# Token shares by expert, a later conversion of weights and an earlier scaling in an attention, MoE and gated-MoE kernel

## The chip, the cores and the metric

The kernel runs on one core of a Trainium2 chip. Its engines are TensorE (PE in the rows, with PEld for its weight loads), VectorE (DVE), ScalarE (ACT), GpSimd (POOL) and SyncE (SP, which only issues transfers). The metric is the device time of one execution in microseconds (us), lower is better.

## The reference

```python
attn = softmax(q @ k.T / 8 + bias) @ v          # 2 batches, 8 heads, 576 positions, 64 wide
x = attn as (1152 tokens, 512)
x = softplus(x @ w_in) @ w_out                  # 512 -> 2048 -> 512
P = exp(logits - max); 8 times: rows, then columns of P scaled to sums 1 and N / E
for e in range(8):                              # E = 8 experts, 512 -> 1024 -> 512
    h = np.maximum(x @ w1[e], 0.0)
    out += P[:, e:e + 1] * (h @ w2[e])
```

## The kernel before

The work after the attention is cut into 40 units of 256 hidden columns each: units 0 to 7 are the first MLP, units 8 to 11 are expert 0, and each further four units are one expert more. The tokens are kept as two blocks of 512 (c = 0, 1) and a rest of 128. Tokens lie along the free dimension, so that the hidden values are [128 hidden, 512 tokens]. float32 accuracy comes from splitting every operand in a high half (rounded to fp32r, a ScalarE copy, `first`) and a low half (the rest, `second`, a subtraction on VectorE or GpSimd). Each product is three matmuls: high with high, low weight with high, high weight with low.

Units 12 to 38 (`fast(u)`) do both the up and the down projection as seven products of 2 x 2 blocks instead of eight (Strassen-Winograd). The up projection takes its products in the order `UP_FAST = (1, 2, 6, 5, 7, 3, 0, 4)` (0 is the rest of 128 tokens, `up_last`). The down projection, `down_fast(u)`, takes seven steps, `at` = 0 to 6, on the blocks B11, T1, T2, B22, T3, B21, T4 of the gated hidden values; T1 to T4 are differences of the B blocks. Products 1 and 2 of unit u + 1 are done inside `down_fast(u)`, and product 6 of unit u + 1 is the first thing after it. The hidden values of a block are multiplied by the tokens' shares for the expert (`pb[c]`, the same row on all 128 partitions) by the VectorE instruction of L880.

The order on each engine is the order of the code; nothing is reordered, and each engine waits where its next instruction has to wait. Between steps 0 and 1 of `down_fast` stand: the ScalarE conversion of the second half of the next unit's up weights (`high(u + 1, 1)`); B21's gating and its high half; at every fourth unit the loads of the next expert's shares; the difference T4; the high and low halves of T3; the low half of B21. Then come T4's halves.

With `by_dma`, a weight piece's conversion is two ScalarE copies (the high half, L730, and its negative into the low half, L734) and a DMA that GpSimd issues (L735) and that adds the float32 source to the low half. In each unit GpSimd issues four such DMAs: wu (this second half), then after `mixd` (L754) wu (the first half of the unit after next) and wd (the down weights), then room (`highs`, the sums of the down weights). All go through one queue, q0. SyncE's transfers (weights, shares) go through q1.

The shares of all tokens and experts, P, are written once to DRAM as the tile `pt` of 72 rows of 128 floats, row t * E + e for token tile t and expert e (`publish`, in unit 11). `share_of` loads 4 of the 9 token tiles of one expert on all partitions: 4 rows of 512 bytes for each. Shares are loaded in `publish` (four transfers: two for expert 1, two for expert 0) and in units 15, 19, 23, 27, 31 and 35 (two each). In unit 12 the sums of expert 0, which were taken without shares, are multiplied by expert 0's shares (`weigh_columns`, L1038: one call on VectorE at n = 3, two on GpSimd at n = 5, one on VectorE in `down_fast`, step 6), where n counts the places in `UP_FAST`.

Of the kernel before, what the change touches and what calls it, by code (L numbers as in the profile page):

```python
# [25 lines left out]
E = 8  # L26
# [87 lines left out]
def attention_moe_moe_kernel(ctx: ExitStack, tc, qT, kT, vN, wpos, w_in, w_out, w_gate, e_w1, e_w2,  # L114
                             psi, logd, rpsi, place, out):
    nc = tc.nc
# [501 lines left out]
    def experts(m0, accp, xr):  # L618
# [6 lines left out]
        U1 = F1 // 256  # L625
        UE = F2 // 256
# [4 lines left out]
        pool = {}  # L631
# [16 lines left out]
        def wd(u):  # L648
            return wds[u % 2]
# [63 lines left out]
        def mix(u):  # L713

            if u >= NU or u in PLAIN:
                return
            w, t = whole2(u, 0), fs[1]

            def at(f, off, *dims):
                return win(f, off, [*dims, [256, 2], [1, 128]])  # L720

            nc.gpsimd.tensor_tensor(out=at(t, 0, [128, 2]), in0=at(w, 128, [512, 2]), in1=at(w, 0, [512, 2]), op=ALU.subtract)
            nc.gpsimd.tensor_tensor(out=at(t, 512), in0=at(w, 640), in1=at(w, 128), op=ALU.subtract)
            nc.gpsimd.tensor_tensor(out=at(t, 640), in0=at(w, 640), in1=at(t, 0), op=ALU.subtract)
            nc.gpsimd.tensor_tensor(out=at(t, 128), in0=at(t, 0), in1=at(t, 128), op=ALU.subtract)  # L725
# [36 lines left out]
        weights = dict(m=rescale, a=convert_a, b=convert_b, c=convert_c, mix=lambda u, k: mix(u), high=high, highd=highd, mixd=mixd, highs=highs)  # L762
        wss, tss, pb = [], [], {}
# [44 lines left out]
        def product(u, n):  # L808

            if n in (1, 2, 5):  # L810
                hold["XYZ"[(1, 2, 5).index(n)]] = bank({1: "t", 2: "tail", 5: "pv"}[n])
            zz = hold[CHAIN[n]]
            xn, wn = PRODUCTS[n]
            k = 0
            for j in range(2):
                for a, b in TRIPS:
                    o = WAT[wn] + 256 * j
                    nc.tensor.matmul(zz, wu(u)[:, a, o:o + 128], xs[xn][b][j], start=(n in (1, 2, 5) and k == 0), stop=(k == 5),  # L818
                                     skip_group_check=True)
                    k += 1  # L820
# [38 lines left out]
        def second(eng, name):  # L859
            t = h[name]  # L860
            eng.tensor_tensor(out=t[:, 1], in0=full[name], in1=t[:, 0].bitcast(F32), op=ALU.subtract)  # L861

        def difference(eng, out, a, b):
            eng.tensor_tensor(out=full[out], in0=full[a], in1=full[b], op=ALU.subtract)
# [111 lines left out]
        def turn_last(u):  # L976
            zt, gl = bank("tail"), hold["gl"]
            for j in range(2):
                nc.tensor.transpose(zt[:, 128 * j:128 * j + 128], gl[:, 128 * j:128 * j + 128], ident)
            t = h["last"] = pool["moe"].tile([128, 2, 256], F32R, tag="hl", bufs=1, name="hl")  # L980
            split_h(u, t, zt[:, 0:256])
            low()

        def down_fast(u):
            product(u + 1, 1)
            begun.add((u + 1, 1))
            banks = hold["sums"]
            for at, (n, x, a, b, (c, i)) in enumerate(DOWN):
                m, o = WDAT[a]
                ws = wss if m else [wd(u)[:, 0], wd(u)[:, 1]]  # L990
                order = [(k, f) for k in range(3) for f in range(2)] if at else [(k, f) for f in range(2) for k in range(3)]
                for k, f in order:
                    wo, ho = ((0, 0), (1, 0), (0, 1))[k]
                    nc.tensor.matmul(banks[x][:, f], ws[wo][:, o + 128 * f:o + 128 * f + 128], h[b][:, ho],  # L994
                                     start=(n in (1, 5, 2) and k == 0), stop=(k == 2), skip_group_check=True)
                if u == U1 + UE and at == 6:
                    weigh_columns(nc.vector, c, i)
                for fs_ in (slice(0, 2),) if at else (slice(0, 1), slice(1, 2)):
                    d = acc[c][:, 2 * i:2 * i + 2][:, fs_]
                    nc.vector.tensor_tensor(out=d, in0=banks[x][:, fs_], in1=d, op=ALU.add)  # L1000
                if at == 0:
                    turn_last(u)
                    if u > U1 + UE:
                        weights["high"](u + 1, 1)
                    later.pop()()
                    if (u + 1 - U1) % UE == 0:
                        shares_of((u + 1 - U1) // UE)
                    difference(nc.gpsimd, "T4", "B21", "T2")
                    first("T3")
                    second(nc.gpsimd, "T3")  # L1010
                    second(nc.gpsimd, "B21")
                if at == (2 if u == U1 + UE else 0):
                    if len(tss) < 3:
                        tss.append(again(2, [128, 2, 512], F32R))
                    h["T4"] = tss[2]
                    first("T4")
                    second(nc.gpsimd, "T4")
                if at == 3:
                    after(u + 1, 1)
                if at == 2:  # L1020
                    r = last_sum(u, "pv")
                if at == 4:
                    product(u + 1, 2)
                    begun.add((u + 1, 2))
                if at == 4:
                    evac(u, 2, 0, r)
                if at == 6:
                    after(u + 1, 2)
                for what, ahead, k in DOWN_JOBS.get(at, ()):
                    if u + ahead < NU:  # L1030
                        weights[what](u + ahead, k)

        def again(n, shape, dtype):
            return (m0 if n < 2 else pool["moe"]).tile(shape, dtype, tag=f"raw{n}", bufs=1, name="raw")

        def weigh_columns(eng, c, i):
            d = acc[c][:, 2 * i:2 * i + 2]
            eng.tensor_tensor(  # L1038
                out=d, in0=d, in1=pb["first", c].rearrange("p (o n) -> p o n", o=1).to_broadcast([128, 2, 512]),
                op=ALU.mult)  # L1040
# [165 lines left out]
        NT = NTOK // 128  # L1206
# [39 lines left out]
        def publish():  # L1246

            tt, sb = bank("t"), raws[2][:, 512:640]
            nc.tensor.transpose(tt[0:NT * E, 0:128], pool["prob"].rearrange("p t e -> p (t e)"), ident)
            nc.vector.tensor_copy(sb[0:NT * E], tt[0:NT * E, 0:128])  # L1250
            nc.sync.dma_start(out=pool["pt"], in_=sb[0:NT * E])
            pb["first", 0], pb["first", 1] = raws[2][:, 0:512], fs[2][:, 512:1024]
            for c in range(2):
                share_of(1, c)
                nc.sync.dma_start(out=pb["first", 1 - c].rearrange("p (t n) -> p t n", n=128), in_=shares(0, 4 * (1 - c), 4))

        def shares(e, t, n):
            src = pool["pt"][:]
            return bass.AP(tensor=src.tensor, offset=src.offset + (t * E + e) * 128, ap=[[0, 128], [128 * E, n], [1, 128]])

        def share_of(e, c):
            pb[c] = pool["moe"].tile([128, 512], F32, tag=("s3", "lgt")[c], bufs=1, name="pb")
            nc.sync.dma_start(out=pb[c].rearrange("p (t n) -> p t n", n=128), in_=shares(e, 4 * c, 4))

        def shares_of(e):
            for c in range(2):
                share_of(e, c)
# [96 lines left out]
        def unit(u):  # L1364
# [62 lines left out]
            if u == U1:  # L1427
                first_up(jobs)
            else:
                for n, p in enumerate(UP_FAST if fast(u) else UP):  # L1430
                    if u == U1 + UE and n == 5:
                        tss.extend(again(k, [128, 2, 512], F32R) for k in range(2))
                        for i in range(2):
                            weigh_columns(nc.gpsimd, 0, 1 - i)
                    if n == 3 and u == U1 + UE:
                        weigh_columns(nc.vector, 1, 0)
                    if n == 6 and u == U1 + UE:
                        weights["high"](u + 1, 1)
                    if n > 1:
                        ask(u, f"q{n - 2}" if n < 5 else f"r{n - 5}")  # L1440
                    if p:
                        do(u, p)
                    else:
                        up_last(u)
                    if u > U1 + UE and p in (6, 5):
                        weights["highs"](u, (6 - p,))
                        if p == 5:
                            weights["mix"](u + 1, 0)
                    jobs(n)
# [222 lines left out]
```

## Time and profile before

| | us |
|---|---|
| median of 3 runs (lowest to highest) | 1184.28 (1183.86 to 1185.43) |
| the profiled execution, its own time | 1183.7 |
| its span, first to last instruction | 1181.9 |
| TensorE busy in it | 1146.2 (97%) |

The span is what the rows below are taken from. The granted TensorE clock was 1.0 throughout. TensorE's matmuls overlap: one is shown for 0.39 us, but the next starts 0.227 us after it. The fast units follow one another at about 22.4 us each.

### The profile page before, as it was taken

How to read it: one execution, taken by the hardware profiler on the slowest of the kernel's cores; microseconds unless marked ns; L12 is line 12 of the kernel's file. 1: busy time of each engine (PE TensorE's matmuls, PEld its weight loads, DVE VectorE, ACT ScalarE, POOL GpSimd, SP SyncE). 2: the span in 40 equal slices, each digit the busy share in tenths (PEclk: the TensorE clock that was granted, in tenths of full speed). 3: DMA queues.
4: the chain of work that ended last, by engine and by line, in shares of the span. 5: the costliest groups of instructions: out<-in, count | busy, mean ns of one | idle time of the engine just before them, and what ended most of it. 6: DMA issues, size and time to landing. Idle time of an engine off the chain costs nothing.

```text
span 1181.9 us, 19793 instructions
## 1 busy us (share of the span) xinstructions
PE 1146.2 (97%) x7289; PEld 958.6 (81%) x7289; DVE 878.2 (74%) x1469; ACT 724.6 (61%) x1190; POOL 840.9 (71%) x858
## 2 busy tenths in 40 slices
PE   5897999999999999999999999999999999999998
PEld 4886999988888887887788887887888887888887
DVE  9986888668888855766777777777777777777773
ACT  8876887865554556335566666665665665666652
POOL 8226777657788874446878878878888887887880
PEclk9999999999999999999999999999999999999999
DMA  5769565022222211126577577567657657658652
GB/s 137 227 172 273 173 199 160 2 71 90 91 90 89 89 54 37 36 36 162 112 154 171 116 152 170 125 136 181 130 123 169 155 114 167 152 121 165 156 110 96
DMA packets 82728, 152.41 MB, mean 129 GB/s; under 512 B 9344, under 2 KB 47304, under 8 KB 82632
## 3 DMA queue, kind: packets, MB, share of 16 engines
q0 software_dynamic: 15984, 58.20, 26.8%
q1 hardware_dynamic: 66072, 92.37, 25.4%
q8 instruction: 57, 0.93, 0.3%
q10 hardware_dynamic: 576, 0.58, 0.2%
q14 instruction: 39, 0.32, 0.1%
HBM read 78.79 MB, written 14.14 MB: 79 GB/s over the span
## 4 chain that ended last, share of the span: by engine, by line
PE 83%; DMA 4%; DVE 4%; issue 3%; POOL 3%; ACT 3%; SPq 0%; DVEq 0%; POOLq 0%; ACTq 0%
PE sum L994 19%; PE t L818 15%; PE sum L1074 10%; PE pv L818 7%; PE op L544 5%; PE pv L1090 4%; PE tail L818 4%; PE pac L269 3%; PE sps L453 3%; PE sum L968 3%; PE tp L503 2%; DMA wu<-f 2%; PE t L836 1%; PE tail L968 1%; DMA room<-f 1%
## 5 line engine op out<-in xcount | busy, mean ns | idle before, releaser
L1000 DVE TENSOR_TENSOR acc<-sum,acc 128x512 f32<-128x512 f32 (+1 forms) x216 | 230.6, 1087 | 91.1 <-PE sum L994 86.7
L818 PE MATMUL t<-room,wu 128*128 128x512 f32 x592 | 160.6, 390 | 0.4 <-DVE u L841 0.4
L1074 PE MATMUL sum<-h,wd 128*128 128x512 f32 x576 | 138.2, 394 | 0.0
L818 PEld LDWEIGHTS t<-room,wu 128*128 128x128 f32 x592 | 111.2, 188 | 23.6 <-DVE u L841 0.9
L1074 PEld LDWEIGHTS sum<-h,wd 128*128 128x128 f32 x576 | 105.5, 188 | 21.9 <-DVE acc L1111 0.4
L818 PE MATMUL pv<-x,wu 128*128 128x512 f32 x444 | 113.1, 390 | 0.0
L730 ACT ACTIVATE wu<-f 128x1024 fp32r<-128x1024 f32 x77 | 81.1, 1054 | 29.6 <-POOL f L725 23.7
L818 PEld LDWEIGHTS pv<-x,wu 128*128 128x128 f32 x444 | 83.1, 188 | 18.0 <-ACT u L846 0.4
L735 POOL DMA_DIRECT2D room<-f x27 | 23.2, 861 | 92.9 <-issue 91.6
L818 PE MATMUL t<-x,wu 128*128 128x512 f32 x296 | 86.4, 392 | 2.2 <-DMA wu<-f 2.2
L861 POOL TENSOR_TENSOR raw<-f,raw 128x512 fp32r<-128x512 f32 x54 | 84.7, 1568 | 0.0
L269 PE MATMUL pac<-bw,m 128*128 128x64 bf16 (+1 forms) x1920 | 66.2, 198 | 18.4 <-DVE bw L241 11.7
L994 PE MATMUL sum<-h,wd 128*128 128x512 f32 x324 | 82.5, 390 | 0.0
L269 PEld LDWEIGHTS <-m 128*128 128x128 bf16 (+1 forms) x1920 | 62.7, 104 | 21.9 <-issue 10.1
L861 POOL TENSOR_TENSOR h<-u,h 128x512 fp32r<-128x512 f32 x55 | 77.8, 1579 | 2.4 <-ACT h L857 2.4
L737 POOL TENSOR_TENSOR wu<-f,wu 128x1024 fp32r<-128x1024 f32 x21 | 53.0, 2526 | 32.6 <-ACT wu L730 31.9
L846 ACT ACTIVATE u<-t 128x512 f32<-128x512 f32 x37 | 22.2, 599 | 85.8 <-PE t L818 85.8
L1111 DVE TENSOR_TENSOR acc<-sum,acc 128x512 f32<-128x512 f32 x80 | 55.1, 689 | 24.7 <-PE sum L1074 24.0
L994 PEld LDWEIGHTS sum<-h,wd 128*128 128x128 f32 x324 | 60.8, 188 | 12.9
L735 POOL DMA_DIRECT2D wu<-f x56 | 49.6, 886 | 26.9 <-ACT h L857 14.7
L994 PE MATMUL sum<-raw 128*128 128x512 f32 x216 | 67.3, 410 | 1.3 <-POOL raw L861 1.3
L818 PEld LDWEIGHTS t<-x,wu 128*128 128x128 f32 x296 | 55.3, 188 | 13.9 <-DMA wu<-f 3.6
(303 smaller groups left out, 3159.3 us busy)
## 6 DMA issues: line engine op xcount, KB each, us to landing
f<-in_e_w_dram SPq DMA_DIRECT2D x128, 256.0 KB, 4.1
wu<-f POOLq DMA_DIRECT2D x56, 512.0 KB, 4.6
wd<-f POOLq DMA_DIRECT2D x28, 512.0 KB, 6.6
room<-f POOLq DMA_DIRECT2D x27, 512.0 KB, 5.3
raw<-in_w_in_dram SPq DMA_DIRECT2D x16, 512.0 KB, 3.6
raw<-in_w_out_dram SPq DMA_DIRECT2D x16, 512.0 KB, 3.6
bias<-wt SPq DMA_DIRECT2D x14, 576.0 KB, 5.9
raw<-in_qT_dram SPq DMA_DIRECT2D x16, 288.0 KB, 5.4
```

Source lines behind the costliest of these rows:

```text
L269: nc.tensor.matmul(pt[0:n, g], lhs, win(w, (k * (ng + 1) + gw) * NC, [[(ng - gw) * NC, 2], [1, NC]]), start=(k == 0), stop=(k == 2))
L544: nc.tensor.matmul(op[:, 0:n], l, r, start=(part == 0 and k == 0), stop=(part == 8))
L730: nc.scalar.activation(hi, src, AF.Copy)
L735: nc.gpsimd.dma_start(out=lo.bitcast(F32), in_=src, accum_op=ALU.add)
L737: nc.gpsimd.tensor_tensor(out=lo, in0=src, in1=hi.bitcast(F32), op=ALU.subtract)
L818: nc.tensor.matmul(zz, wu(u)[:, a, o:o + 128], xs[xn][b][j], start=(n in (1, 2, 5) and k == 0), stop=(k == 5), skip_group_check=True)
L861: eng.tensor_tensor(out=t[:, 1], in0=full[name], in1=t[:, 0].bitcast(F32), op=ALU.subtract)
L968: nc.tensor.matmul(zr[:, 0:256], xl[:, b, k], wu(u)[:, a, 256 * k:256 * k + 256], start=(n == 0), stop=(n == 3 * KT - 1))
L994: nc.tensor.matmul(banks[x][:, f], ws[wo][:, o + 128 * f:o + 128 * f + 128], h[b][:, ho], start=(n in (1, 5, 2) and k == 0), stop=(k == 2) ...
L1000: nc.vector.tensor_tensor(out=d, in0=banks[x][:, fs_], in1=d, op=ALU.add)
L1074: nc.tensor.matmul(s, lhs, rhs, start=(n == 0), stop=(n == 5))
L1111: nc.vector.tensor_tensor(out=d, in0=o, in1=d, op=ALU.add)
```

## The change

Three edits. (1) `pt` is laid out by expert (row e * NT + t, NT = 9), so that four token tiles of one expert are one run of 2048 bytes; the write of `pt` is spread accordingly, and the twelve loads of the six later experts as well as the four in `publish` read single runs. (2) In `down_fast`, `high(u + 1, 1)` is moved behind B21's gating, the loads of shares, the difference T4 and both halves of T3; it stands ahead of B21's low half. (3) In unit 12 the two GpSimd calls of `weigh_columns` are issued at n = 3, behind the VectorE one, instead of at n = 5.

```diff
                 if at == 0:
                     turn_last(u)
-                    if u > U1 + UE:
-                        weights["high"](u + 1, 1)
                     later.pop()()
                     if (u + 1 - U1) % UE == 0:
                         shares_of((u + 1 - U1) // UE)
                     difference(nc.gpsimd, "T4", "B21", "T2")
                     first("T3")
                     second(nc.gpsimd, "T3")
+                    if u > U1 + UE:
+                        weights["high"](u + 1, 1)
                     second(nc.gpsimd, "B21")
...
-            nc.sync.dma_start(out=pool["pt"], in_=sb[0:NT * E])
+            dst = pool["pt"][:]
+            nc.sync.dma_start(out=bass.AP(tensor=dst.tensor, offset=dst.offset, ap=[[128, NT], [128 * NT, E], [1, 128]]),
+                              in_=sb[0:NT * E])
...
-                nc.sync.dma_start(out=pb["first", 1 - c].rearrange("p (t n) -> p t n", n=128), in_=shares(0, 4 * (1 - c), 4))
+                nc.sync.dma_start(out=pb["first", 1 - c], in_=shares(0, 4 * (1 - c), 4))
...
-            return bass.AP(tensor=src.tensor, offset=src.offset + (t * E + e) * 128, ap=[[0, 128], [128 * E, n], [1, 128]])
+            return bass.AP(tensor=src.tensor, offset=src.offset + (e * NT + t) * 128, ap=[[0, 128], [1, 128 * n]])
...
-            nc.sync.dma_start(out=pb[c].rearrange("p (t n) -> p t n", n=128), in_=shares(e, 4 * c, 4))
+            nc.sync.dma_start(out=pb[c], in_=shares(e, 4 * c, 4))
...
                     if u == U1 + UE and n == 5:
                         tss.extend(again(k, [128, 2, 512], F32R) for k in range(2))
+                    if n == 3 and u == U1 + UE:
+                        weigh_columns(nc.vector, 1, 0)
                         for i in range(2):
                             weigh_columns(nc.gpsimd, 0, 1 - i)
-                    if n == 3 and u == U1 + UE:
-                        weigh_columns(nc.vector, 1, 0)
```

## Rows read from the trace of the kernel before

**Rows 1.** The page: busy time by engine; DMA issues (KB, median us to landing).
```profile
PE 1146.2 (97%) x7289; PEld 958.6 (81%) x7289; DVE 878.2 (74%) x1469; ACT 724.6 (61%) x1190; POOL 840.9 (71%) x858
...
wu<-f POOLq DMA_DIRECT2D x56, 512.0 KB, 4.6
```
**Rows 2.** Waits of TensorE's matmuls, 550 to 1182 us (total us, times, longest).
```profile
PE t L818 <- DMA wu<-f: 2.2, 3, 1.0
PE sum L994 <- POOL raw L861: 2.0, 2, 1.3
```
**Rows 3.** Waits of TensorE's weight loads, 566 to 1150 us.
```profile
PEld sum L994 <- POOL h L861: 6.8, 24, 0.6
...
PEld sum L994 <- DMA room<-f: 3.3, 8, 0.7
```
**Rows 4.** Two stretches of unit 19, the last columns clock, DMA share, GB/s.
```profile
713.50:720.50 7.00, 7.00 (x32) 5.55 (x31) 5.38 (x6) 5.25 (x8) 6.63 (x7) 1.00 0.42 117
710.50:713.50 3.00, 3.00 (x16) 2.27 (x15) 2.30 (x5) 1.88 (x4) 3.00 (x4) 1.00 0.89 302
```
**Rows 5.** DMA issues, 0.5 to 1.2 us: one row of 2304 bytes to all partitions.
```profile
v<-in_psi_dram ACTq DMA_DIRECT2D x1, 288.0 KB, 3.5
```
**Rows 6.** DMA issues, 713.5 to 720.5 us (unit 19).
```profile
wu<-f POOLq DMA_DIRECT2D x1, 512.0 KB, 9.7
```
**Rows 7.** Timeline of TensorE (start, us, idle before), units 12, 19 and 20.
```profile
556.16 0.73 PE L994 MATMUL sum<-raw 128*128 128x512 f32 x2 [1.28 <-POOL raw L861]
...
724.56 1.19 PE L818 MATMUL t<-x,wu 128*128 128x512 f32 x4 [0.98 <-DMA wu<-f]
...
741.50 0.61 PE L994 MATMUL sum<-h,room 128*128 128x512 f32 x2
741.98 0.73 PE L994 MATMUL sum<-h,raw 128*128 128x512 f32 x2
742.55 0.63 PE L818 MATMUL tail<-room,wu 128*128 128x512 f32 x2
...
746.67 1.52 PE L818 MATMUL t<-x,wu 128*128 128x512 f32 x6
```
**Rows 8.** Timeline of GpSimd, unit 20.
```profile
736.30 1.55 POOL L864 TENSOR_TENSOR u<-v,u 128x512 f32<-128x512 f32 x1
738.48 0.88 POOL L735 DMA_DIRECT2D wu<-f  x1 [0.62 <-ACT h L857]
739.09 1.59 POOL L864 TENSOR_TENSOR f<-u,f 128x512 f32<-128x512 f32 x1
740.34 2.83 POOL L861 TENSOR_TENSOR h<-u,h 128x512 fp32r<-128x512 f32 x2
```
**Rows 9.** Timeline of ScalarE, unit 20.
```profile
736.88 1.05 ACT L734 ACTIVATE wu<-f 128x1024 fp32r<-128x1024 f32 x1
737.82 1.14 ACT L857 ACTIVATE h<-u 128x512 fp32r<-128x512 f32 x2
```
**Rows 10.** Timeline of VectorE, units 12 and 20.
```profile
542.69 1.21 DVE L1038 TENSOR_TENSOR acc<-acc,f 128x1024 f32<-128x1024 f32 x1
...
564.88 1.44 DVE L1038 TENSOR_TENSOR acc<-acc,f 128x1024 f32<-128x1024 f32 x1
...
736.96 0.68 DVE L880 SCALAR_TENSOR_TENSOR u<-t,pb 128x512 f32<-128x512 f32 x1
```
**Rows 11.** DMA, 748.5 to 756.5 us: packets, MB, share; issues.
```profile
q0 software_dynamic: 411, 1.55, 105.4%
...
room<-f POOLq DMA_DIRECT2D x1, 512.0 KB, 5.2
```
**Rows 12.** DMA issues, 661 to 662 us (unit 17).
```profile
room<-f POOLq DMA_DIRECT2D x1, 512.0 KB, 6.1
```
**Rows 13.** Timeline of GpSimd, unit 12.
```profile
549.25 4.77 POOL L1038 TENSOR_TENSOR acc<-acc,raw 128x1024 f32<-128x1024 f32 x2 [2.75 <-DMA raw<-pt]
...
554.55 1.56 POOL L861 TENSOR_TENSOR raw<-f,raw 128x512 fp32r<-128x512 f32 x1
```

## The prediction

> **What bounds the kernel now.** The page comes first: TensorE is busy for 1146.2 of 1181.9 us [rows 1], so an edit on another engine can win only the moments in which TensorE stands still for what that edit makes sooner. I then read who TensorE waits for, once for its matmuls and once for its weight loads, because a matmul of 0.39 us overlaps the next and hides a short wait that the weight loads show. The matmuls' list has two entries that the change can touch: 2.2 us in three waits for the DMA that completes the up weights, and 2.0 us in two waits for a low half made by GpSimd [rows 2]. The weight loads' list adds 24 waits, 6.8 us, for T3's low half on GpSimd, and 8, 3.3 us, for the room DMA [rows 3]. The timelines place them. The waits for the up weights fall in units 19, 23 and 31, all units that load shares; the GpSimd pair is unit 12, around the scaled sums; T3's is in nearly every fast unit; room's is in some.
>
> A shown idle is less than what it costs. Matmuls start 0.227 us apart and are shown for 0.39, so a wait costs 0.16 more than its idle; and the two starts after it are 0.57 apart (741.98 to 742.55) where two starts take 0.455, another 0.11 [rows 7]. I add 0.27 for each idle.
>
> **Edit 1, the shares' layout.** In unit 19 SyncE's weight loads move at 302 GB/s until 713.5, and then the shares' stretch moves at 117 with the DMA engines 42% busy, for 7 us [rows 4]. The wu DMA that GpSimd issues meanwhile lands after 9.7 us [rows 6], against the usual 4.6 [rows 1], and TensorE stands still at 724.56 [rows 7]. Six units have such a load, three of them a wait. With one run of 2048 bytes for each partition the packets fall to a quarter. The nearest row is the load of psi, one row of 2304 bytes to all partitions: 288 KB landed in 3.5 us [rows 5]. The bounds: two shares (512 KB) at 302 GB/s take 1.7 us; two landings of 3.5 one after the other take 7 and win nothing. I take 3.5 + 1.7 = 5.2 us, counted from 713.5, where the shares' packets begin: q1 is empty by 718.7 at the latest. TensorE asks for the weights at 724.56 - 0.98 - 0.16 = 723.4, 23.7 us ahead of the same matmul in unit 20 (747.1, below); edit 2 makes GpSimd issue the wu DMA at 741.28 - 23.7 = 717.6, so it hardly queues, and even if it began at 718.7 it would land by 718.7 + 4.6 = 723.3. The three waits go: 2.2 + 3 x 0.27 = 3.0 us. Below: nothing. What is late next in these units is what is late in all, T3's low half.
>
> **Edit 3, the sums of expert 0.** At 549.25 GpSimd has stood for 2.75 us for the last of the four shares that `publish` loads; it multiplies for 4.77, issues a wu DMA, and only at 554.55 starts T2's low half [rows 13], for which TensorE waits 1.28 us [rows 7]. All of GpSimd's steps down to T4's low half follow in a chain, hence the second wait. Issued at n = 3, the two multiplications stand ahead of B22's low half, one 1.25 us step, instead of behind it. What counts is when the share lands. TensorE wants T2's low half at 556.16 - 1.28 - 0.16 = 554.72; back from there 1.56 for the pass, 0.61 for the DMA issue, 1.25 for B22 (both steps from [rows 8]) and 4.77 for the multiplications, they must begin by 546.5. Four shares are 1 MB: 9.0 us at 117 GB/s, 3.5 at 302 [rows 4]; that is 5.5 us sooner, 543.8. So both waits go, 2.0 + 2 x 0.27 = 2.5, less 0.2 because B21's gating on VectorE comes no sooner, so that T4 gains less than T2: 2.3 us. Bounds: 2.5, and a loss of 1.3 if the share lands at 549.25 as now, for B22's 1.25 us step then stands ahead of T2's. So edit 3 lives on edit 1.
>
> **Edit 2, the conversion behind T3.** ScalarE now converts the weights until 737.9 and then B21 and T3 [rows 9]. After the change it waits for B21's gating, which ends at 736.96 + 0.68 = 737.64 [rows 10], does B21 and T3 from 737.7 (0.54 each), then the two weight copies, 0.95 apart, from 738.7 to 740.7. T4's high half follows at 740.6, in time. GpSimd before: T3's difference at 736.30, the DMA issue 0.55 us after the copy's end, T4's difference at 739.09, T3's and B21's low halves from 740.34, in steps of 1.25, T4's low half from 742.84 [rows 8]. After: T4's difference at 737.7, T3's low half at 738.95, done at 740.5; the DMA issue at 740.7 + 0.55 = 741.28; 0.61 later B21's low half (741.89), T4's at 743.14. Three consequences.
>
> First, T3's low half is 1.4 us sooner. TensorE's pairs of matmuls start 0.455 apart; around it they are 0.48 and 0.57 [rows 7], so each of the 24 waits costs 0.14: 24 x 0.14 = 3.4 us won.
>
> Second, the second half of the up weights is asked for 2.8 us later and lands at 741.28 + 4.6 = 745.9. Its first low-half matmul is the third of the product at 746.67, at 747.1, and 0.3 sooner in weight loads and lost waits [rows 7]: about 0.9 us left, enough.
>
> Third, GpSimd is 743.14 - 742.84 = 0.30 us later for all that follows, and that is not free. The two wu and wd transfers and room's run in one queue without a pause: q0 has 105% of 16 engines from 748.5 to 756.5 [rows 11]. So room lands 0.30 later though it is issued as before, and TensorE comes 0.14 sooner. Room usually takes 5.2 us from its issue [rows 11]; in unit 17 it takes 6.1 [rows 12], and in the eight units that wait they wait 0.41 on average, so the weight loads' edge is near 5.7 and the matmuls' near 5.9. Usual units go to 5.2 + 0.44 = 5.64 and stay inside; the eight late ones lose 0.44 each, 3.5 us. The cover of the other units is then 0.26 us. Bounds of the price: 0, if the late landings have a cause that does not move with the queue, and more than 3.5 if GpSimd's delay is larger than 0.30. I take 3.5, since the queue shows no pause. Edit 2 is thus -3.4 + 3.5 = +0.1.
>
> **Sum.** -3.0 - 2.3 + 0.1 = -5.2 us on the profiled execution's 1183.7 (span 1181.9 and 1.8 around it) = 1178.5. The median of the runs is 0.6 above it: 1179.1.
>
> **Rivals.** (a) Room's edge is passed by all (slower). If GpSimd's delay is s instead of 0.30, 18 usual units lose s + 0.14 - 0.7 and eight lose s + 0.14; against the 8.7 us won this decides from s = 0.68. At s = 0.9 it is 6.1 + 8.3 - 8.7 = +5.7: 1190.0. For it: the DMA issue is shown for 0.88 where I count 0.61 [rows 8], and the wait for ScalarE sums four latencies. Against: each of them is read from a row. 0.09.
>
> (b) The shares land no sooner, the layout does not do what it says: edit 1 wins 0, edit 3 loses 1.3, edit 2 costs 0.1: +1.4, 1185.7. For it: all partitions read the same bytes of DRAM, before and after. Against: psi's 3.5 us [rows 5] and the 42% busy engines [rows 4]. 0.08.
>
> The Trainium skill (DMA: Bandwidth & Descriptors, Specifications) puts line rate at runs of 512 bytes and more; by that rule the old layout lost nothing and (b) would come about. The trace does not agree, with 117 GB/s in such runs against 302 in longer ones [rows 4].
>
> (c) Room's late landings do not move with the queue: 3.5 us more are won, 1175.6. For it: only eight units are late, so something else makes them so. 0.20.
>
> (d) In unit 12 VectorE's multiplication, 1.21 us at 542.69, now runs beside GpSimd's. The one at 564.88, beside a GpSimd pass, took 1.44 [rows 10]. If it is held until both GpSimd calls end, VectorE is 2.2 us late with its next steps, B11's low half comes 0.6 to 0.8 too late, and edit 3 wins 1.5: 1179.9. 0.08.
>
> The Trainium skill (SBUF — State Buffer, Who interferes with whom) says that a VectorE instruction with two SBUF inputs and a GpSimd one that reads SBUF exclude each other for a whole instruction; by that rule (d) would come about, and the 0.23 us of the row above agrees with it.
>
> **How the numbers follow.** Forecast 0.55 (its own range, 1177.0 to 1181.5: the residual of each term), (a) 0.09, (b) 0.08, (c) 0.20, (d) 0.08. The range takes the forecast, (c) and (d): 1175.2 to 1182.0. 0.2%, 2.4 us, is about what a measurement of this kernel can tell from no change, so faster means below 1181.9: 0.51 of the forecast, all of (c), 0.06 of (d): 0.77. Slower means above 1186.7: most of (a) and a little of (b): 0.09. The rest, 0.14, is the same.
>
> **What would show it.** Right: no wait for wu in units 19, 23 and 31; a wu DMA there landing in under 6 us; GpSimd's L1038 in unit 12 beginning before 546.5 and no wait for `raw`; no weight-load wait for h on GpSimd; the wu issue some 2.8 us later within its unit. Room's waits grown from 3.3 us to about 7 if the third consequence is right, unchanged if (c) is. Wrong: L1263's transfers as long as before; room waits in all 26 units; a wait for wu in units without shares.

## The result, and the profile after

The changed kernel takes 1174.61 us (median of 4 runs, 1174.23 to 1175.37), the kernel before 1184.64 in 4 runs beside it: a ratio of 0.9916, 95% interval 0.9899 to 0.9933. The direction is as predicted, the size is not: 10.0 us were won where 5.2 were forecast, and the time lies 0.6 us below the range. The profiled execution took 1175.37, with a span of 1173.6, 8.3 less than before. The other 1.7 us are spread between executions: the profiled one is 0.9 below the median before and 0.8 above it after.

The page, busy time by engine and the queue of SyncE's transfers (packets, MB, share):

```profile
PE 1141.2 (97%) x7289; PEld 960.9 (82%) x7289; DVE 879.1 (75%) x1469; ACT 724.6 (62%) x1190; POOL 841.1 (72%) x858
...
q1 hardware_dynamic: 59925, 92.37, 25.3%
```

The same bytes go in 6147 fewer packets (66072 before): sixteen loads on 128 partitions with one run instead of four are 16 x 128 x 3 = 6144 fewer.

The waits of TensorE's matmuls, 550 to 1182 us, and then of its weight loads, 566 to 1150 us, of the changed kernel (us in total, times, longest):

```profile
PE sum L994 <- DMA room<-f: 1.0, 3, 0.6
PE pv L968 <- DVE u L880: 0.3, 1, 0.3
```
```profile
PEld sum L994 <- DMA room<-f: 4.9, 9, 1.0
PEld sum L994 <- issue: 4.9, 18, 0.3
```

Against [rows 2, 3]: the waits for the up weights, for GpSimd's low half in unit 12 and for T3's low half are all gone. Room alone is left, and it has grown from 3.3 us in 8 waits to 4.9 in 9.

Two stretches of unit 19 behind the shares' issue (last columns clock, DMA share, GB/s), and the DMA issues of 709.5 to 716 us (KB, us to landing):

```profile
710.00:713.00 3.00, 3.00 (x14) 2.30 (x13) 3.00 (x5) 1.75 (x3) 3.00 (x4) 1.00 0.81 294
712.00:716.00 4.00, 4.00 (x20) 3.29 (x19) 2.64 (x3) 4.00 (x6) 3.60 (x4) 1.00 0.34 114
```
```profile
pb<-pt SPq DMA_DIRECT2D x2, 256.0 KB, 3.9
wu<-f POOLq DMA_DIRECT2D x1, 512.0 KB, 4.6
```

The first stretch still holds the end of the weight loads, so its 294 GB/s is not the rate of the shares, and it does not answer to the 117 of [rows 4]. In the trace the shares' own packets run from about 711.5 to 714.5, 3 us where they took 7 before; after 714.5 the queue is all but empty, which is why the second stretch shows only 114. The wu DMA lands after the usual 4.6 us where it took 9.7 [rows 6]. GpSimd's and VectorE's timelines in unit 12, which answer to [rows 10, 13]:

```profile
545.39 4.78 POOL L1038 TENSOR_TENSOR acc<-acc,raw 128x1024 f32<-128x1024 f32 x2 [3.89 <-DMA raw<-pt]
550.13 1.28 POOL L861 TENSOR_TENSOR h<-v,h 128x512 fp32r<-128x512 f32 x1
551.37 0.83 POOL L735 DMA_DIRECT2D wu<-f  x1
551.98 1.54 POOL L861 TENSOR_TENSOR raw<-f,raw 128x512 fp32r<-128x512 f32 x1
```
```profile
542.58 1.22 DVE L1038 TENSOR_TENSOR acc<-acc,f 128x1024 f32<-128x1024 f32 x1
```

The last share came at 545.39, ahead of the limit of 546.5 that the prediction set, and T2's low half (the last line of GpSimd's) begins 2.6 us sooner than in [rows 13]. VectorE's multiplication had ended before GpSimd's began.

Unit 20 on GpSimd, ScalarE and TensorE, which answers to [rows 7 to 9]; the unit begins at 725.51 (729.68 before):

```profile
733.62 1.34 POOL L864 TENSOR_TENSOR f<-u,f 128x512 f32<-128x512 f32 x1
734.88 1.33 POOL L861 TENSOR_TENSOR h<-u,h 128x512 fp32r<-128x512 f32 x1
736.86 0.88 POOL L735 DMA_DIRECT2D wu<-f  x1 [0.65 <-ACT wu L734]
737.47 1.60 POOL L861 TENSOR_TENSOR h<-u,h 128x512 fp32r<-128x512 f32 x1
738.73 1.60 POOL L861 TENSOR_TENSOR raw<-f,raw 128x512 fp32r<-128x512 f32 x1
```
```profile
734.57 1.04 ACT L730 ACTIVATE wu<-f 128x1024 fp32r<-128x1024 f32 x1
735.52 1.04 ACT L734 ACTIVATE wu<-f 128x1024 fp32r<-128x1024 f32 x1
```
```profile
737.35 0.62 PE L994 MATMUL sum<-h,room 128*128 128x512 f32 x2
737.80 0.61 PE L994 MATMUL sum<-h,raw 128*128 128x512 f32 x2
738.25 1.30 PE L818 MATMUL tail<-room,wu 128*128 128x512 f32 x5
```

T3's pair on TensorE now starts 0.45 after the pair ahead of it and is followed after 0.45; both gaps were longer in [rows 7]. On GpSimd the order is as predicted (T4's difference, T3's low half, the DMA issue, B21's and T4's low halves). But T4's low half begins 738.73 - 725.51 = 13.22 us into the unit, where it was 742.84 - 729.68 = 13.16 [rows 8]: 0.06 later, not 0.30. The copy ends at 735.52 + 1.04 = 736.56 and the issue begins 0.30 after it; in [rows 8, 9] it was 0.55. This is so in every unit from 13 to 37: 0.55 before (0.83 in unit 24), 0.30 after.

One table, worked out from the starts of each unit's first matmul in the traces, holds for all that follows (us; one profiled execution of each kernel, of the changed one two):

```
                                 unit 12   19     23     31    22 others: median, sum   units 12-37
before                            24.79  23.70  23.17  23.45     22.43   494.26         589.37
after                             22.31  22.26  22.36  22.26     22.27   492.07         581.26
after, another execution          22.59  22.24  22.30  22.24     22.26   491.00         580.37
layout alone                      22.29  22.41  22.42  22.45     22.41   494.28         583.85
later conversion alone            25.15  26.23  22.35  23.08     22.27   491.82         588.63
earlier scaling alone             26.31  24.51  22.50  24.07     22.42   494.53         591.92
layout + scaling                  22.41  22.44  22.39  22.39     22.43   494.00         583.64
layout + later conversion         22.27  22.24  22.27  22.24     22.26   491.56         580.58
after, runs of 512 B, 528 apart   27.11  22.24  22.35  22.26     22.26   491.35         585.31
after, runs of 512 B, 4096 apart  27.53  24.75  23.03  22.47     22.26   493.35         591.13
after, wu ahead of mixd           22.26  22.83  22.26  22.52     22.45   498.15         588.02
after, conversion behind B21      22.40  22.24  22.26  22.26     22.26   490.95         580.11
after, only the issue moved       22.64  22.24  22.24  22.24     22.26   490.33         579.69
```

So the 8.1 us of units 12 to 37 are 2.5 in unit 12, 3.4 in units 19, 23 and 31, and 2.2 in the 22 others. The second execution of the changed kernel gives 9.0, so single profiles differ by about a microsecond.

### The profile page after: what moved, and what is told of

Its sections match the earlier page's. It is cut to its first block, busy times and chain, and to the rows that moved or that the text cites. A ratio compares the mean times of both kernels' runs of the same rounds, so it can differ in the third digit from the quotient of the medians.

```text
span 1173.6 us, 19768 instructions
## 1 busy us (share of the span) xinstructions
PE 1141.2 (97%) x7289; PEld 960.9 (82%) x7289; DVE 879.1 (75%) x1469; ACT 724.6 (62%) x1190; POOL 841.1 (72%) x858
## 4 chain that ended last, share of the span: by engine, by line
PE 86%; DMA 4%; DVE 3%; issue 3%; ACT 2%; POOL 1%; SPq 0%; DVEq 0%; ACTq 0%; POOLq 0%
PE sum L994 21%; PE t L818 15%; PE sum L1074 10%; PE pv L818 7%; PE op L544 5%; PE pv L1090 4%; PE tail L818 4%; PE pac L269 3%; DMA room<-f 3%; PE sps L453 3%; PE sum L968 3%; PE tp L503 2%; PE t L836 1%; PE tail L968 1%; PE sum L1053 1%
## 5 line engine op out<-in xcount | busy, mean ns | idle before, releaser
L818 PE MATMUL t<-room,wu 128*128 128x512 f32 x592 | 160.6, 390 | 0.4 <-DVE u L841 0.4
L818 PEld LDWEIGHTS t<-room,wu 128*128 128x128 f32 x592 | 111.2, 188 | 23.6 <-DVE u L841 0.8
L818 PE MATMUL pv<-x,wu 128*128 128x512 f32 x444 | 113.1, 390 | 0.0
L818 PEld LDWEIGHTS pv<-x,wu 128*128 128x128 f32 x444 | 83.0, 188 | 18.0 <-ACT u L846 0.4
L818 PE MATMUL t<-x,wu 128*128 128x512 f32 x296 | 85.5, 390 | 0.0
L861 POOL TENSOR_TENSOR h<-u,h 128x512 fp32r<-128x512 f32 x55 | 81.1, 1479 | 2.4 <-ACT h L857 2.4
L470 ACT ACTIVATE p<-p,sm 128x576 f32<-128x576 f32 x72 | 55.7, 774 | 16.3 <-DVE sm L466 15.3
```

Source lines behind the costliest of these rows:

```text
L470: nc.scalar.activation(p, p, AF.Exp, bias=sm[:, o:o + 1], scale=-1.0, accum_out=sm[:, 2 + o:3 + o])
```

## The experiments

**Each edit alone, and pairs.** The edits are those of the diff above, applied singly to the kernel before.

> The layout of the shares alone, the order and the scaling as before. Theory 1 (the layout carries both the share units and unit 12): no wait for wu in units 19, 23 and 31 (3.0 us), and in unit 12 the last share lands at about 545.4 as with all three edits, while GpSimd is free for the sums only at 546.5, so both waits there go too (2.5 us): 5.5 us faster than before, about 1179.1. Rival (the forecast's division, the scaling must also be issued sooner): 3.0 us faster, about 1181.6, with the two waits in unit 12 still there.

> The later conversion alone, layout and scaling as before. Theory 1 (room's price is 1.4 us, as the trace after all three edits has it, not 3.5): T3's waits go (3.3), room's grow by 1.4, the waits for wu in units 19, 23 and 31 stay: 1.9 us faster, about 1182.7. Rival, the forecast's price: no change, about 1184.7. Second rival (the conversion hides more than T3's wait and is what the forecast missed): 4 to 5 us faster, about 1180.

> The earlier scaling alone, layout and order as before. Theory 1: GpSimd still waits for the last share until about 549.2, and B22's low half now stands behind the multiplications: T2's low half is 1.25 us later, 1.3 us slower than before, about 1185.9. Rival (the place in the queue is what held the sums back): 2.3 us faster, about 1182.3.

> Layout and earlier scaling, the conversion as before. Theory 1: the same as the layout alone, within 0.3 us, about 1179.1, since the share lands only 1.1 us before GpSimd would have come to the sums anyhow. Rival (forecast's division): 2.3 us faster than the layout alone.

> Layout and later conversion, the scaling as before. Theory 1 (the scaling's place is worth nothing once the share lands early): as after the change, within 0.5 us. Rival (it is worth the 2.3 us that the forecast gave it): 2.3 us slower than after the change, and two waits in unit 12.

> The kernel after the change once more, to weigh its median against that of before over more runs. If the profiled executions tell all of it: 8.3 us faster, about 1175.9. If the gain is the 10.0 us of the first medians, the loads of shares cost the kernel before more in most executions than in the profiled one: about 1174.5.

Measured (us, median; ratio to the kernel before on the same chip, 95% interval):

| kernel | us | ratio |
|---|---|---|
| layout alone | 1179.01 | 0.9961 [0.9948, 0.9973] |
| later conversion alone | 1182.12 (11 executions; a twelfth took 2934.73) | 0.9985 [0.9973, 0.9996] |
| earlier scaling alone | 1186.29 | 1.0022 [1.0012, 1.0032] |
| layout + scaling | 1178.43 | 0.9954 [0.9940, 0.9969] |
| layout + later conversion | 1174.75 | 0.9920 [0.9908, 0.9932] |
| all three, again | 1175.35 | 0.9922 [0.9910, 0.9935] |

The repeat of all three edits is 8.3 us below the kernel before by the medians and 9.2 by the ratio, whose interval, 7.7 to 10.7 us, holds both figures that were expected of it.

Waits of TensorE's weight loads with the layout alone, then of its matmuls with the later conversion alone, and a line of TensorE's timeline in unit 19 of the latter:

```profile
PEld sum L994 <- POOL h L861: 6.3, 22, 0.6
...
PEld sum L994 <- DMA room<-f: 3.7, 8, 1.1
```
```profile
PE t L818 <- DMA wu<-f: 2.8, 3, 2.0
PE sum L994 <- POOL raw L861: 2.0, 2, 1.3
```
```profile
725.89 2.68 PE L818 MATMUL pv<-x,wu 128*128 128x512 f32 x6
```

The layout alone takes the waits of the share units and those of unit 12 as well (22.29 in the table, with the scaling still at its old place), and leaves T3's. The later conversion alone takes T3's wait, but in unit 19 the wu DMA, asked for later, then stands in the slow shares and TensorE waits 2.05 us instead of 0.98. Behind that wait the granted clock was 0.50 from 726.0 to 729.4 us, 1.2 GHz, and six matmuls are shown for 2.68 us instead of 1.52; so unit 19 takes 2.5 us more than before (26.23 and 23.70), not 1.1. By the ratios the later conversion is worth 0.0015 without the layout (1.8 us) and 0.0032 (beside the scaling) to 0.0041 (without it) on top of it, 3.8 to 4.9 us. The intervals of the single ratios are wide for this difference; the unit sums point the same way, 0.7 us without the layout and 2.4 to 3.3 with it. The scaling adds nothing measurable to the layout, with the later conversion (0.9920 to 0.9922) or without (0.9961 to 0.9954), and alone it costs 2.6 us. There GpSimd waits for the share as long as before and B22's step now stands behind the multiplications too; timeline of GpSimd, and of TensorE:

```profile
549.43 4.77 POOL L1038 TENSOR_TENSOR acc<-acc,raw 128x1024 f32<-128x1024 f32 x2 [7.92 <-DMA raw<-pt]
```
```profile
557.57 0.73 PE L994 MATMUL sum<-raw 128*128 128x512 f32 x2 [2.78 <-POOL raw L861]
```

2.78 where it was 1.28 [rows 7], 1.5 more; the prediction gave 1.3 for a share that lands no sooner. The rest is in units 19 and 31 of the table (0.8 and 0.6 longer, while unit 23 is 0.7 shorter): the two kernels differ in nothing there.

**What makes the shares' transfer slow.** Two kernels keep all three edits and the order by expert, but pad the rows of `pt`, so that a load is four runs of 512 bytes again: 528 bytes apart, and then 4096 apart, as they lay before the change.

```diff
-            pool["pt"] = dp.tile([E * NTOK // 128, 128], F32, name="pt")
+            pool["pt"] = dp.tile([E * NTOK // 128, 132], F32, name="pt")       # second kernel: 1024
...
-            ... offset=src.offset + (e * NT + t) * 128, ap=[[0, 128], [1, 128 * n]])
+            ... offset=src.offset + (e * NT + t) * 132, ap=[[0, 128], [132, n], [1, 128]])
```

> After the change, with 16 bytes of space behind each row of 128 floats of pt: the shares still lie by expert and side by side, but each partition reads four runs of 512 bytes again. Theory (the length of a run sets the rate): the shares take as long as before the change, the waits for wu in the units that load shares come back, and unit 12 loses as the earlier scaling alone did: 5 to 8 us slower than after the change. Rival (what cost time was the spread of the four rows over DRAM, 4096 bytes apart): as after the change.

> The changed kernel with its shares again read in four runs of 512 bytes for each partition, as in the kernel whose rows are padded to 528 bytes, but here the four pieces lie 4096 bytes apart, as they did before the change. In the one with 528 bytes between pieces the shares of a unit landed after 5.0 us (6.8 before, 4.3 after the change), TensorE waited for no up weights in units 19, 23 and 31, and all of its loss, 4.8 us, was in unit 12. Theory A, the distance between the pieces counts: the shares land after about 6.8 us again, and two or three waits for the up weights come back in units 19, 23 and 31; unit 12 loses as before or more. 1182.5 to 1185, that is 3 to 5 us above the kernel with 528 bytes between pieces. Theory B, only the length of a run counts: landing 5.0 us, no wait for the up weights, 1179 to 1180.5.

Measured: 1179.61 us, 0.9958 [0.9946, 0.9971], with 528; 1185.28 us, 1.0005 [0.9995, 1.0014], with 4096. Both send the same packets on q1 (66069). Landing of the shares' loads from 600 us on, first of the changed kernel, then with 528, then with 4096 bytes between pieces:

```profile
DMA to landing us min/median/max: 3.3/4.3/4.7
```
```profile
DMA to landing us min/median/max: 3.9/5.0/5.2
```
```profile
DMA to landing us min/median/max: 5.9/6.8/7.4
```

The kernel before has 6.8 here. So pieces of 512 bytes with 16 bytes between them cost 0.7 us of a landing against one run, and a distance of 4096 bytes 1.8 more. Whether the 0.7 is for the shorter run or for pieces that no longer start on multiples of 512 bytes was not separated. The waits of TensorE's matmuls with 4096 bytes:

```profile
PE t L818 <- DMA wu<-f: 3.3, 3, 2.2
PE t L818 <- DVE tail L841: 2.8, 1, 2.8
```

The waits for the up weights are back with the distance and only with it, in units 19, 23 and 27; with 528 bytes no such wait is left, and all that is lost lies in unit 12, where four loads run at once (27.11 against 22.31 in the table, 4.8 us; the medians differ by 5.0). With 4096 bytes unit 12 loses 5.2 us at another place: VectorE stands 6.24 us, until 549.15, for a share that its own multiplication needs, and TensorE waits 2.78 us for VectorE's next step (second line). The ratio of this kernel, 1.0005, is what is left of the other two edits without the layout (0.9985 and 1.0022). The second run was expected at 1182.5 to 1185 and came 0.3 above. The theory behind the first, that the length of the runs is what the layout changes, fits unit 12 and falls for the share units. Unit 12 shows one thing more, timeline of TensorE and a stretch of it (the third column from the end is the granted clock) with 528 bytes:

```profile
557.56 0.74 PE L994 MATMUL sum<-raw 128*128 128x512 f32 x2 [2.74 <-POOL raw L861]
558.14 2.53 PE L1090 MATMUL pv<-wd,hl 128*128 128x512 f32 x6
```
```profile
557.50:560.50 3.00, 2.94 (x9) 2.31 (x10) 1.23 (x1) 1.14 (x2) 3.00 (x4) 0.65 0.63 117
```

After the wait of 2.74 us the granted clock is 0.65 over three microseconds, a mean of stretches at 1.2 and at 2.4 GHz, and six matmuls are shown for 2.53 us where six take 1.52 in [rows 7]. With the scaling alone the same wait, 2.78, was followed by a granted clock of 1.00. From the first of these six matmuls to the first of the next product (`tail`, L818) it is 5.73 us here (558.14 to 563.87) and 4.10 there (558.14 to 562.24): the lower clock cost 1.6 us. Over the whole unit it is 0.8 (27.11 and 26.31), since there a second wait of 0.69 follows that is gone here.

**What room waits for.** In the first kernel (from the changed one) the wu DMA of the first half goes ahead of `mixd`, so that wu and wd are no longer side by side in the queue. In the second the moved conversion goes behind B21's low half as well, so that GpSimd no longer idles ahead of the issue. The third is the second with the scaling at its old place. The fourth has ScalarE's two copies back ahead of B21's gating and moves only GpSimd's DMA issue behind T3's low half.

```diff
# first
-        DOWN_JOBS = {1: (("mixd", 1, 0),), 3: (("high", 2, 0),), 4: (("highd", 1, 0),)}
+        DOWN_JOBS = {3: (("high", 2, 0), ("mixd", 1, 0)), 4: (("highd", 1, 0),)}
# second and third
                     second(nc.gpsimd, "T3")
-                    if u > U1 + UE:
-                        weights["high"](u + 1, 1)
                     second(nc.gpsimd, "B21")
+                    if u > U1 + UE:
+                        weights["high"](u + 1, 1)
# fourth
                     turn_last(u)
+                    if u > U1 + UE:
+                        half = wu(u + 1)[:, :, 1024:2048]
+                        nc.scalar.activation(half[:, 0], fs[1], AF.Copy)
+                        nc.scalar.activation(half[:, 1], fs[1], AF.Copy, scale=-1.0)
...
-                        weights["high"](u + 1, 1)
+                        nc.gpsimd.dma_start(out=half[:, 1].bitcast(F32), in_=fs[1], accum_op=ALU.add)
                     second(nc.gpsimd, "B21")
```

> After the change, with the wu DMA for the unit after next issued ahead of mixd instead of behind it; wd is issued as late as now. Theory A (room lands where the backlog of q0 leaves it, nothing else counts): room lands about 0.9 sooner, its waits go, 2 to 2.5 us faster than after the change. Rival B (wd then lands at about 1.0 within its unit, SyncE's next loads start at once and share the DMA engines with room, as in units 13, 20 and 32 of the kernel before, where room took 5.6 instead of 5.2): room lands at 5.9 or later in every unit, no gain to 1 us slower.

> After the change, with the conversion of the second weight half one step later still, behind B21's low half. GpSimd then fills the 0.65 us that it stands ahead of that DMA, and issues wu and wd 0.6 sooner. Theory A (room's landing follows the queue): room lands near 5.2 as in unit 14 after the change, its waits go from nine to two or three, 2 to 2.5 us faster than after the change; the wu lands at 16.5 within its unit, wanted at 17.0, no wait. Rival C (the late landings have a cause that does not move with the queue): room's waits as they are, no change.

> The variant with the conversion behind B21's low half, with the scaling of the first sums where it was before the change. Theory (the scaling's place is worth nothing once the shares land early): as that variant, 1173.3 within 0.6 us. Rival: 1 to 2 us slower.

> After the change, but ScalarE's two copies of the second weight half stand where they stood before it, ahead of B21 and T3; only GpSimd's DMA issue is moved behind T3's low half. Theory (what held T3 back was GpSimd's wait for ScalarE at that issue, not ScalarE's time): T3's waits stay away, the issue finds the copies done, GpSimd loses its idle 0.65 us, wu and wd go out about 0.8 sooner than after the change, and room lands as in the variant behind B21: 1.5 to 2.5 us faster than after the change. Rival (T3's high half on ScalarE is what was late): T3's waits come back, 24 of them, 3 to 4 us slower than after the change.

Measured: first 1182.89 us, 0.9988 [0.9978, 0.9999]; second 1173.33, 0.9908 [0.9895, 0.9921]; third 1174.49, 0.9912 [0.9897, 0.9928]; fourth 1173.13, 0.9905 [0.9891, 0.9918]. Waits of TensorE's weight loads for room in the first, the second and the fourth:

```profile
PEld sum L994 <- DMA room<-f: 13.6, 20, 2.9
```
```profile
PEld sum L994 <- DMA room<-f: 2.3, 4, 0.9
```
```profile
PEld sum L994 <- DMA room<-f: 1.4, 3, 0.7
```

The first kernel is 7.5 us slower than the changed one, worse than either of its two theories allowed, though room is issued at the same place. What moved is wd: in unit 20 it lands 0.27 us into the unit instead of 2.79. It frees the buffers that SyncE's next weight loads wait for, and these start 0.17 us after room's issue instead of 2.7 us after it. Room then shares the DMA engines with them and lands after 6.2 us in the median (5.5 in the changed kernel). More than half of what the profile loses is one unit, 35, with 26.30 us: room lands there after 8.3 us, beside a packet of the instruction queue that took 2.7 us (more on these below), TensorE's matmuls wait 2.45, and the granted clock is 0.50 from 1072.0 to 1075.4. The second kernel has no idle ahead of the DMA issue. Its GpSimd in unit 20, and that of the fourth:

```profile
733.94 2.57 POOL L861 TENSOR_TENSOR h<-u,h 128x512 fp32r<-128x512 f32 x2
736.44 0.88 POOL L735 DMA_DIRECT2D wu<-f  x1
737.05 1.60 POOL L861 TENSOR_TENSOR raw<-f,raw 128x512 fp32r<-128x512 f32 x1
```
```profile
733.58 1.34 POOL L861 TENSOR_TENSOR h<-u,h 128x512 fp32r<-128x512 f32 x1
734.83 0.93 POOL L1014 DMA_DIRECT2D wu<-f  x1
735.44 1.64 POOL L861 TENSOR_TENSOR h<-u,h 128x512 fp32r<-128x512 f32 x1
736.71 1.62 POOL L861 TENSOR_TENSOR raw<-f,raw 128x512 fp32r<-128x512 f32 x1
```

In both, GpSimd and with it the wu and wd transfers are sooner (T4's low half begins 12.5 us into the unit, 13.22 in the changed kernel), and room's waits fall. The fourth is the fastest of all, 10.6 us below the kernel before on its chip (1183.71), and the second is as fast within the intervals. Against the changed kernel the second gains 2.0 us by the medians on one chip and the fourth 1.3 to 2.0 by the ratios, about what was expected; the intervals overlap, so the size of this gain is not sharp. T3's waits stay away in the fourth. So where GpSimd's issue stands is what T3 gains from; ScalarE's place is not needed for it. The third was expected within 0.6 us of the second; it is 1.2 above by the medians and 0.0004 by the ratios, whose intervals hold both. That the scaling is worth nothing is thus not refuted, and not shown to better than a microsecond.

**Which units wait for room.** Before and after the change the same seven units do: 17, 22, 23, 28, 29, 34 and 35. Beside them there is unit 26 before, and units 13 and 24 after, the last for 0.2 us; in unit 26 and unit 13 room is issued 0.7 and 0.4 us later than in most. In these seven, and in no other unit from 13 on, a packet of queue q8, `instruction` in the page of the changed kernel, falls in the first 2.7 us, while room is on its way:

```profile
q8 instruction: 57, 0.93, 0.3%
```

Such a packet is 16 KB and holds a DMA engine for 0.9 to 1.8 us. Room takes 6.0 to 6.5 us from its issue in these units; in the others it takes up to 5.9, but for unit 13 after the change, 6.3. No kernel moved these packets, so that they make room late is a coincidence in time that was not tested. The queue counts beside them: in the second and fourth kernel room lands after 5.5 to 6.2 us in the same seven units.

## Why the prediction was wrong

Its terms against the table. The 25 units but unit 12 lose the same 0.16 in the median, 22.43 - 22.27, which is booked for T3; room is what is left of the 22 others, 22 x 0.16 - 2.2 = 1.3, half of it in unit 13 (22.45 before, 22.95 after, so 0.50 + 0.16):

| term | predicted | measured |
|---|---|---|
| up weights, units 19, 23, 31 (edit 1) | -3.0 | 3 x 0.16 - 3.44 = -3.0 |
| unit 12 (edit 3) | -2.3 | -2.5 |
| T3's waits (edit 2) | -3.4 | 25 x 0.16 = -4.0 |
| room (edit 2) | +3.5 | 1.3 - 0.7 = +0.7 (rounded) |
| room in unit 13 | not in the sum | +0.7 |
| sum | -5.2 | -8.1 |

**The step that failed is "Third", the price of room's edge: +3.5 us predicted, +0.7 measured.** Of the 2.9 us of difference 2.8 are this term; the 0.8 more that T3 and unit 12 won and the 0.7 that unit 13 lost nearly cancel. The direction was right: room's waits grow when GpSimd is later, and fall when GpSimd is sooner (second and fourth kernel). The term was mis-sized because its input was: GpSimd is 0.06 us later behind the issue, in nearly every unit, not 0.30. The prediction carried over the 0.55 us between a copy's end and the issue from [rows 8, 9], but after the change the gap is 0.30. With 0.06 + 0.16 = 0.22 instead of 0.44 for each of the eight late units its own formula gives 1.8, still too much: in the seven units that wait in both profiles room lands 0.10 us later from its issue (6.11 and 6.21 on average), and 7 x 0.10 is the 0.7. Why not the full 0.22 is open. Booked with the same 0.16, the second execution of the changed kernel gives 0.3 and the later conversion alone 1.1, so the price is about a microsecond or less. The split between T3 and room rests on the median; what does not is edit 2 as a whole, +0.1 predicted and -4.0 + 0.7 = -3.3 measured.

Where the shorter gap comes from is open. The traces show one thing that differs: before, the wait for the copy stands in an instruction of its own (its record ends at 737.98 in unit 20, and the issue begins 0.50 us later); after the change the issue itself waits for the copy.

**Unit 13** waits for room after the change and did not before. It is not edit 2's doing: the unit takes 23.01 us with the layout alone, and 22.23 with the later conversion alone. In the second execution of the changed kernel it takes 22.29, while unit 12 takes 22.59. The prediction asked of edits 1 and 3 what they win, and not what becomes late behind them.

**T3** was taken from two gaps around one pair, 0.14 in 24 units; the whole unit shows 0.16, in 25: 0.6 us more.

**Edit 1** came out as reckoned, 3.0 us, by the step named (the wu DMA no longer queues behind the shares). The reason given, longer runs, was only part: pieces 528 bytes apart would have done for these three units. The 117 GB/s of [rows 4], which the prediction read as the rate of 512-byte runs, is for the greater part the rate of pieces 4096 bytes apart: 528 apart, such runs move at 179 GB/s with the DMA engines 67% busy (716.0 to 718.5 us of that kernel). The Trainium skill (DMA: Bandwidth & Descriptors, Latency and other measured facts) has a row on it: copies whose row pitch in DRAM is a large power of two run at as little as half their rate, and padding a pitch by 4 KiB brings the rate back, while 192 bytes did not; the page calls the aliasing of memory channels behind it an inference. Its pitches are 512 KiB and more and here it is 4 KiB, so the row's sizes are not tested, and no run here pads a pitch of 4096 bytes; its direction agrees, 6.8 us at 4096 bytes and 5.0 at 528 with the same runs. The mechanism in the memory stays open here too.

**Edit 3** has the right number for the wrong edit. The share's landing alone ends the waits of unit 12; with the layout the old place of the scaling is early enough. "Edit 3 lives on edit 1" was right, and the other half, that with edit 1 it brings 2.3, was wrong: the limit of 546.5 was worked out for the new place, and what the old place would do with a share at 543.8 was not asked. At the old place B22's step runs in GpSimd's idle time while the share is under way, and the multiplications begin without a wait; layout and later conversion together, timeline of GpSimd in unit 12:

```profile
544.91 1.28 POOL L861 TENSOR_TENSOR h<-v,h 128x512 fp32r<-128x512 f32 x1 [3.61 <-ACT h L857]
546.16 4.77 POOL L1038 TENSOR_TENSOR acc<-acc,raw 128x1024 f32<-128x1024 f32 x2
...
551.49 1.57 POOL L861 TENSOR_TENSOR raw<-f,raw 128x512 fp32r<-128x512 f32 x1
```

T2's low half begins at 551.49 there and at 551.98 with the new place, 5.27 and 5.56 us into the unit: the earlier scaling even comes 0.3 us later to what TensorE asks for.

**The rivals.** (a) did not come: room waits in 9 units, not 26. (b) did not come; the kernel with pieces 4096 bytes apart, whose shares land as late as before, is what (b) describes, and takes 1185.28 where the prediction said 1185.7. That they agree is luck: (b) let edit 2 cost 0.1 and edit 3 cost 1.3, and alone the one won 1.8 us and the other cost 2.6. (c) gave the nearest time, 1175.6. Half of its reason is seen: the late units are those in which an instruction packet falls. The other half, that their landings do not move with the queue, is what the second and fourth kernel speak against. (d) was not put to the test, since in no kernel VectorE's multiplication and GpSimd's two overlapped.

## What to carry to other kernels

Price a moved instruction by where the engine's next fixed step begins, not by the sum of gaps read from the old order; a gap between two engines belongs to that order. When several edits meet in one stage, ask of each what it would be worth if the others were already there: here the layout had won what the scaling was credited with, and the later conversion was worth more with it than without (3.8 to 4.9 us against 1.8). When a wait falls in some units and not in others, look in the trace for what those units have in common before pricing it for all. A transfer that lands sooner can be a loss, if what it frees starts another one beside the transfer that is on the path.

## What the runs showed of the hardware

The same number of 512-byte packets was slower by 1.8 us of 6.8 a landing when a partition's pieces lay 4096 bytes apart instead of 528. Of the six waits of TensorE over 2 us from unit 12 on in all the profiles, four went with a fall of the granted clock to 0.50 at their end or within 1.2 us behind it, for over three microseconds (2.05, 2.45, 2.74 and 2.78 us long), and two with none (2.22 and 2.78). The lower clock cost 1.6 us behind the wait of 2.74. A software DMA issue began 0.30 us after the ScalarE copy that it waited for in one order of the code and 0.55 after it in the other, in nearly every unit. The 512 KB transfer for `room` took 6.0 to 6.5 us to land in the seven units in which a 16 KB packet of the instruction queue fell beside it, and up to 5.9 in the others but one.
